# A three-layer float16-pair kernel: GpSimd's elementwise work moved to VectorE and ScalarE

## The chip, the cores and the metric

The kernel runs on one core of one Trainium2 chip. The metric is the device time of one execution in microseconds (us); less is better. Engines are named as in the profile: PE (TensorE matmul), DVE (VectorE), ACT (ScalarE), POOL (GpSimd), SP (SyncE, which here only issues DMAs).

## The reference

The inputs are q, k, v (8 x 8 heads x 576 tokens x 64), a norm weight, and two pairs of float64 weight matrices (512 x 2048 and 2048 x 512).

```python
kv = einsum('bhsd,bhse->bhde', k, v)
out = einsum('bhsd,bhde->bhse', q, kv)
x = out / sqrt(mean(out * out) + 1e-6) * g_norm        # 4608 tokens x 512
h = x @ w_in;   x = (h * sigmoid(1.702 * h)) @ w_out   # layer 0
h = x @ w2_in;  x = (h - tanh(h)) @ w2_out             # layer 1
```

## The kernel before

**Numbers as pairs.** Every operand of the two dense layers is split into a float16 high part and a float16 low part; a product is three float16 matmuls (high-high, high-low, low-high) of 128 x 128 by 128 x 288. The weights arrive as float64 words and are put together on the chip: `words` scales the upper word (line 153 on ACT for layer 0, line 155 on POOL for layer 1), then three DVE instructions (lines 158, 159, 161) shift and merge the bits. ACT casts the result to the high part (lines 187, 212), and `low_part` (line 177) subtracts it from the float32 value.

**Strassen's scheme.** From the second superblock on, each matrix product is done with seven block products in place of eight (Winograd's form). That needs four sums of the weight quadrants: `four` (lines 170 to 173). In layer 0 the sums are made after the first superblock, from the pairs that are already there: `sums_in` and `sums_out` first add high and low part again (lines 228, 246: the pair recombination), then call `four`, cast (lines 234, 256) and subtract. In layer 1 `conv1` does words, sums, cast and low part for 32 pieces and keeps the pairs in DRAM. The moving operand needs three differences and one more in place, in `xprep` (line 315, four instructions per half), then its pairs (lines 325 on ACT, 328 on DVE).

**Superblocks.** 4608 tokens are eight superblocks of 576 per layer. Superblock 0 of layer 0 runs without Strassen's scheme: `m1_plain` (lines 723 to 725) while weights are still being converted by `conv0` in small places of SBUF (st, jt, cbk, xo, gt), then `m2_plain` (lines 756 to 758, operands by lines 739 on ACT and 740 on DVE, in a ring of three). `sums` begins inside `m2_plain`. Superblocks 1 to 7 and all of layer 1 run `m1` (lines 520 to 522; copies out of PSUM at 553 on ACT, additions at 558 on DVE, activations at 527/531) and `m2` (lines 692 to 694; operands by 581 on DVE, 595 on ACT, 601 on DVE; results by 646 on ACT and 640 on DVE).

**Side work.** Beside superblock n of layer 0 runs the attention of superblock n+1: `front` (matmuls 382, 390, 413; squares 401 on ACT, their fp32r copy 404 and remainder 405 on DVE), `roots`, `newton`, and `back` (matmul 448, product 452 on DVE, then `xprep`). `xprep` of superblocks 2 to 6 does line 315 on POOL. From superblock 2 on `conv1` is a second strand. POOL also issues the DMAs of `conv1` and the stores of the results.

**What sets the order.** Side work is written as generators that `tick` advances by fixed rates at each step of the main work; the framework then schedules the program by its own timeline. Each engine executes its queue strictly in that order: an instruction that waits holds all behind it. The rates are not touched by the change, but the order within each queue comes out differently.

## Time and profile before

| | |
|---|---|
| median of three runs | 1568.98 us (1566.72 to 1574.88) |
| span of the profiled execution | 1565.8 us |
| PE, DVE, ACT, POOL busy | 94%, 77%, 58%, 32% of the span |
| POOL busy, all but 25 us of it in the first half | 501.9 us |
| layer 1 begins (first line 520 of its first superblock) | 815.6 us |

The profile gives the time of the profiled execution as its span, from the first to the last instruction; the median of the runs is 3.2 us above it. Busy shares are averages over very unlike stages: superblock 0 (to 188 us), superblock 1 with the rest of the weight sums (to 306 us), superblocks 2 to 7 with attention and `conv1` (to 816 us), and layer 1.

### The profile page before, as it was taken

The page shows a single profiled execution, that of the slowest core. Times are in us where ns is not written, and L with a number is a line of the kernel's source. Part 1 is how long each engine was busy: PE and PEld are TensorE (multiplying, and loading weights), DVE is VectorE, ACT ScalarE, POOL GpSimd, SP SyncE. Part 2 cuts the span into 40 slices and gives each one's busy share as a digit, 9 for nine tenths or more (in the row PEclk, how much of TensorE's full clock was granted, in tenths as well). Part 3 has the DMA queues.
Part 4 walks back from the last instruction along what each step waited for, and adds up shares of the span by engine and source line. Part 5 has one row for each costly group of instructions (what it writes and reads, how often), then busy time and mean ns, then how long its engine had stood idle before and what let it go on. Part 6 is the DMA issues. An engine that isn't in the chain of part 4 may idle for free.

```text
span 1565.8 us, 29411 instructions
## 1 busy us (share of the span) xinstructions
PE 1467.6 (94%) x11508; PEld 1157.2 (74%) x11508; DVE 1205.1 (77%) x2037; ACT 909.4 (58%) x1979; POOL 501.9 (32%) x565
## 2 busy tenths in 40 slices
PE   6969689989999898999999999999999999999998
PEld 5747467767777677777777777777777777777777
DVE  6996998488587696896967777787878786878585
ACT  6655376565665565666646555655655565656463
POOL 2599842165675665745440000000000000000000
PEclk7979899999999999999999999999999999999999
DMA  8673422617647457366475615243343425150604
GB/s 304 186 211 103 142 94 96 237 41 233 217 126 229 152 161 249 105 230 217 122 234 181 234 62 167 76 139 119 116 135 98 144 77 166 52 168 18 202 15 152
DMA packets 88907, 235.34 MB, mean 150 GB/s; under 512 B 9664, under 2 KB 41536, under 8 KB 88768
## 3 DMA queue, kind: packets, MB, share of 16 engines
q1 hardware_dynamic: 75264, 184.30, 36.8%
q0 software_dynamic: 13504, 49.16, 9.3%
q8 instruction: 90, 1.47, 0.4%
q14 instruction: 49, 0.40, 0.1%
HBM read 191.48 MB, written 41.94 MB: 149 GB/s over the span
## 4 chain that ended last, share of the span: by engine, by line
issue 31%; PE 26%; DVE 21%; DMA 8%; POOL 8%; ACT 4%; SPq 1%; DVEq 0%; POOLq 0%; ACTq 0%
DVE gt L581 4%; DVE jt L601 4%; PE X L520 3%; PE X L522 2%; PE X L521 2%; PE X L694 2%; PE X L693 2%; PE X L692 2%; DVE xo L328 2%; DVE mscratch L558 2%; POOL cbk L170 1%; DMA wod<-cbk 1%; PE Y L692 1%; PE Y L693 1%; PE Y L694 1%
## 5 line engine op out<-in xcount | busy, mean ns | idle before, releaser
L601 DVE SCALAR_TENSOR_TENSOR jt<-gt,jt 128x576 f16<-128x576 f32 x420 | 335.2, 808 | 110.1 <-ACT jt L595 106.3
L595 ACT ACTIVATE jt<-gt 128x576 f16<-128x576 f32 x420 | 282.2, 681 | 140.3 <-PE X L694 50.4
L520 PE MATMUL X<-xo,wi 128*128 128x288 f16 x960 | 276.1, 288 | 9.8 <-ACT mscratch L553 6.9
L692 PE MATMUL X<-jt,st 128*128 128x288 f16 x960 | 274.0, 286 | 4.0 <-ACT mscratch L646 3.0
L522 PE MATMUL X<-xo,wi 128*128 128x288 f16 x960 | 275.9, 287 | 0.0
L521 PE MATMUL X<-xo,wi 128*128 128x288 f16 x960 | 275.8, 287 | 0.0
L693 PE MATMUL X<-jt,st 128*128 128x288 f16 x960 | 274.4, 286 | 0.4 <-DVE jt L601 0.4
L694 PE MATMUL X<-jt,st 128*128 128x288 f16 x960 | 274.3, 286 | 0.0
L521 PEld LDWEIGHTS <-wi 128*128 128x128 f16 x1680 | 165.2, 98 | 73.7 <-issue 30.6
L520 PEld LDWEIGHTS <-wi 128*128 128x128 f16 x1680 | 165.1, 98 | 48.3 <-ACT wi L234 4.4
L553 ACT COPY mscratch<-X 128x288 f32<-128x288 f32 x360 | 140.5, 394 | 101.9 <-PE X L522 88.4
L693 PEld LDWEIGHTS <-st 128*128 128x128 f16 x1680 | 164.4, 98 | 47.3 <-issue 4.4
L637 POOL DMA_DIRECT2D outT<-mscratch x28 | 20.0, 714 | 558.9 <-DVE mscratch L640 519.8
L692 PEld LDWEIGHTS <-st 128*128 128x128 f16 x1680 | 164.4, 98 | 46.9 <-DMA st<-wod 4.8
L694 PEld LDWEIGHTS <-st 128*128 128x128 f16 x1680 | 164.4, 98 | 45.6 <-issue 3.5
L522 PEld LDWEIGHTS <-wi 128*128 128x128 f16 x1680 | 165.2, 98 | 42.6
L581 DVE TENSOR_TENSOR gt<-gt 128x576 f32<-128x576 f32 x240 | 188.2, 796 | 1.3 <-ACT gt L527 0.5
L520 PE MATMUL Z<-xo,wi 128*128 128x288 f16 x480 | 138.1, 288 | 18.6 <-DVE mscratch L558 14.6
L558 DVE TENSOR_TENSOR mscratch<-Z,mscratch 128x288 f32<-128x288 f32 x240 | 108.0, 451 | 44.2 <-ACT mscratch L553 26.8
L693 PE MATMUL Y<-jt,st 128*128 128x288 f16 x480 | 136.8, 286 | 2.2 <-DVE jt L601 2.0
L521 PE MATMUL Z<-xo,wi 128*128 128x288 f16 x480 | 138.3, 288 | 0.0
L522 PE MATMUL Z<-xo,wi 128*128 128x288 f16 x480 | 138.2, 288 | 0.0
(255 smaller groups left out, 2970.1 us busy)
## 6 DMA issues: line engine op xcount, KB each, us to landing
st<-wod SPq DMA_DIRECT2D x210, 512.0 KB, 4.7
scratch<-att SPq DMA_DIRECT2D x28, 928.0 KB, 6.6
x2d<-mscratch POOLq DMA_DIRECT2D x32, 288.0 KB, 5.1
scratch<-x2d SPq DMA_DIRECT2D x32, 288.0 KB, 5.8
cbk<-w_out POOLq DMA_DIRECT2D x32, 256.0 KB, 4.2
cbk<-w_in POOLq DMA_DIRECT2D x32, 256.0 KB, 4.3
outT<-mscratch POOLq DMA_DIRECT2D x28, 288.0 KB, 4.8
wid<-cbk POOLq DMA_DIRECT2D x16, 448.0 KB, 3.7
```

The source lines that it names most:

```text
L328: nc.vector.scalar_tensor_tensor(out=dst[:, a:b, 1, :], in0=src, scalar=SX, in1=dst[:, a:b, 0, :], op0=ALU.mult, op1=ALU.subtract)
L520: nc.tensor.matmul(out=out, lhsT=wh, rhs=xh, start=fresh and kt == 0, stop=False, skip_group_check=k)
L521: nc.tensor.matmul(out=out, lhsT=wh, rhs=xl, start=False, stop=False, skip_group_check=k)
L522: nc.tensor.matmul(out=out, lhsT=wl, rhs=xh, start=False, stop=kt == 1, skip_group_check=k)
L553: main(nc.scalar.copy(out=b.ap, in_=x))
L558: main(nc.vector.tensor_tensor(out=b.ap, in0=add[0], in1=b.ap, op=ALU.add))
L581: tt = lambda o, a, b: main(nc.vector.tensor_tensor(out=G[:, :, o, :], in0=G[:, :, a, :], in1=G[:, :, b, :], op=ALU.subtract))
L595: main(nc.scalar.activation(out=j[:, :, 0, :], in_=GT[STEPS2[i][1]][:, :, QD[STEPS2[i][0]], :], func=AF.Copy, scale=SX))
L601: main(nc.vector.scalar_tensor_tensor(out=j[:, :, 1, :], in0=GT[STEPS2[i][1]][:, :, QD[STEPS2[i][0]], :], scalar=SX, in1=j[:, :, 0, :], op ...
L692: nc.tensor.matmul(out=out, lhsT=wh, rhs=xh, start=a, stop=False, skip_group_check=k)
L693: nc.tensor.matmul(out=out, lhsT=wh, rhs=xl, start=False, stop=False, skip_group_check=k)
L694: nc.tensor.matmul(out=out, lhsT=wl, rhs=xh, start=False, stop=z, skip_group_check=k)
```

## The change

All arithmetic leaves POOL, which keeps its few set-up copies and the DMA issues:

- scaling of words (line 155, 32 of 128x512) goes to ACT, as it already was for layer 0;
- `four`, `low_part` and the pair recombination (lines 170 to 173, 177, 228, 246) go to DVE wherever they were on POOL;
- the four subtractions of `xprep` for superblocks 2 to 6 (line 315, 40 of 128x288) go to DVE;
- the fp32r copy of the squares (line 404, 32 of 128x576 on DVE) is replaced by a second Square on ACT that writes fp32r from PSUM (64 of 128x288). Line 405 keeps its subtraction.

DVE's queue goes from 2039 to 2359 instructions, ACT's from 1981 to 2077, POOL's from 570 to 185. PE executes the same matmuls.

```diff
     def words(l, raw, wb):
...
-        if l == 0:
-            nc.scalar.activation(out=av, in_=rf[:, :, 1], func=AF.Copy, scale=2.0 ** -111)
-        else:
-            nc.gpsimd.tensor_scalar(out=av, in0=rf[:, :, 1], scalar1=2.0 ** -111, scalar2=None, op0=ALU.mult)
+        nc.scalar.activation(out=av, in_=rf[:, :, 1], func=AF.Copy, scale=2.0 ** -111)
...
-    def four(Q, E, l=0, e=None):
+    def four(Q, E, l=0):
...
-        tt = (e or nc.gpsimd).tensor_tensor
+        tt = nc.vector.tensor_tensor
...
-    def low_part(d, src, on_pool):
-        e = nc.gpsimd if on_pool else nc.vector
-        e.tensor_tensor(out=d[..., 1, :], in0=src, in1=d[..., 0, :], op=ALU.subtract)
+    def low_part(d, src):
+        nc.vector.tensor_tensor(out=d[..., 1, :], in0=src, in1=d[..., 0, :], op=ALU.subtract)
...
-            low_part(d, x, True)
+            low_part(d, x)
...
-            low_part(d, B[:, 1:8], k % 2)
+            low_part(d, B[:, 1:8])
...
-            nc.gpsimd.tensor_tensor(out=Q[:, h], in0=d[:, h, 0:4, 0, :], in1=d[:, h, 0:4, 1, :], op=ALU.add)
+            nc.vector.tensor_tensor(out=Q[:, h], in0=d[:, h, 0:4, 0, :], in1=d[:, h, 0:4, 1, :], op=ALU.add)
...
-                nc.gpsimd.tensor_tensor(out=x, in0=d[:, :, 0, :], in1=d[:, :, 1, :], op=ALU.add)
+                nc.vector.tensor_tensor(out=x, in0=d[:, :, 0, :], in1=d[:, :, 1, :], op=ALU.add)
...
-            nc.gpsimd.tensor_tensor(out=Q, in0=r[:, :, 0, :], in1=r[:, :, 1, :], op=ALU.add)
+            nc.vector.tensor_tensor(out=Q, in0=r[:, :, 0, :], in1=r[:, :, 1, :], op=ALU.add)
...
-        low_part(r, Q, on_pool)
+        low_part(r, Q)
...
-        tt = lambda o, a, b: e.tensor_tensor(out=o, in0=a, in1=b, op=ALU.subtract)
+        tt = lambda o, a, b: nc.vector.tensor_tensor(out=o, in0=a, in1=b, op=ALU.subtract)
...
                 nc.scalar.activation(out=sq[:, c], in_=A[j][:, 0:H], func=AF.Square)
+                nc.scalar.activation(out=shr[:, c], in_=A[j][:, 0:H], func=AF.Square)
                 nc.scalar.activation(out=og[:, c], in_=A[j][:, 0:H], func=AF.Copy, scale=gsc)
             yield
-            nc.vector.tensor_copy(out=shr, in_=sq)
             nc.vector.tensor_tensor(out=slr, in0=sq, in1=shr.bitcast(F32), op=ALU.subtract)
...
-                yield from xprep(xbs[b, kt], ex, dst[:, kt], nc.gpsimd if 2 <= b <= 6 else nc.vector)
+                yield from xprep(xbs[b, kt], ex, dst[:, kt])
```

Blank lines replace comments in the changed file, and lines are gone, so its numbers run a little lower: 155, 156, 158 are the word instructions 158, 159, 161; 167 to 170 the four sums 170 to 173; 173 the low part 177; 224 and 242 the recombination 228 and 246; 310 is line 315, 323 is 328, 400 is 405, 447 is 452, 553 is 558, 576 is 581, 596 is 601, and 735 is 740.

**Place one: DVE's queue while the last pieces of W_out are converted, beside `m1_plain`** (xo, st, jt and cbk are places of pieces, wi and st the kept pairs). Before:

```order
L158 TENSOR_SCALAR xo_72<-xo_72 128x512
L161 SCALAR_TENSOR_TENSOR cbk<-cbk 128x512 x2
L158 TENSOR_SCALAR xo_72<-xo_72 128x512
L159 SCALAR_TENSOR_TENSOR xo_72<-xo_72 128x512 x2
L161 SCALAR_TENSOR_TENSOR xo_72<-xo_72 128x512 x2
L158 TENSOR_SCALAR st<-st 128x512
L158 TENSOR_SCALAR jt<-jt 128x512
L159 SCALAR_TENSOR_TENSOR st<-st 128x512
L159 SCALAR_TENSOR_TENSOR jt<-jt 128x512
L161 SCALAR_TENSOR_TENSOR st<-st 128x512
```

with the change:

```order
L158 SCALAR_TENSOR_TENSOR xo_72<-xo_72 128x512
L400 TENSOR_TENSOR sq_104<-scratch,sq_103 128x576
L156 SCALAR_TENSOR_TENSOR st<-st 128x512
L155 TENSOR_SCALAR jt<-jt 128x512
L173 TENSOR_TENSOR wi_67<-cbk,wi_67 128x3x128
L173 TENSOR_TENSOR st<-cbk,st 128x128
L173 TENSOR_TENSOR wi_68<-xo_72,wi_68 128x3x128
L173 TENSOR_TENSOR st<-xo_72,st 128x128
L158 SCALAR_TENSOR_TENSOR st<-st 128x512
L173 TENSOR_TENSOR wi_68<-xo_72,wi_68 128x3x128
L156 SCALAR_TENSOR_TENSOR jt<-jt 128x512
L173 TENSOR_TENSOR st<-xo_72,st 128x128
```

The low parts, 128x384 and 128x128 for each piece, now stand between the shifts of the next pieces. From the third to the fourth line 740 (735) DVE has 42 instructions in the old queue and 79 in the new one.

**Place two: DVE's queue at the end of `m2_plain`** (scratch holds the attention of superblock 1, xo its operands; gt is the GELU of superblock 0; line 740 or 735 on gt_76 is the last operand of `m2_plain`). Before:

```order
L452 TENSOR_TENSOR scratch<-AT_88,scratch 128x288
L452 TENSOR_TENSOR scratch<-AT_89,scratch 128x288
L177 TENSOR_TENSOR cbk<-cbk 128x4x128
L315 TENSOR_TENSOR scratch<-scratch 128x288 x2
L740 SCALAR_TENSOR_TENSOR jt<-gt_76,jt 128x2x288
L315 TENSOR_TENSOR scratch<-scratch 128x288
L328 SCALAR_TENSOR_TENSOR xo_72<-scratch,xo_72 128x2x288 x3
L740 SCALAR_TENSOR_TENSOR jt<-gt_76,jt 128x2x288
L328 SCALAR_TENSOR_TENSOR xo_72<-scratch,xo_72 128x288
```

with the change:

```order
L224 TENSOR_TENSOR cbk<-wi_63 128x512
L173 TENSOR_TENSOR cbk<-cbk 128x4x128
L735 SCALAR_TENSOR_TENSOR jt<-gt_76,jt 128x2x288
L310 TENSOR_TENSOR scratch<-scratch 128x288
L224 TENSOR_TENSOR st<-wi_65 128x512
L224 TENSOR_TENSOR cbk<-wi_64 128x512
L167 TENSOR_TENSOR st<-st 128x128
L447 TENSOR_TENSOR scratch<-AT_88,scratch 128x288
L224 TENSOR_TENSOR jt<-wi_66 128x512
L224 TENSOR_TENSOR cbk<-wi_64 128x512
L447 TENSOR_TENSOR scratch<-AT_89,scratch 128x288
```

Before, the attention's products (452) and differences (315) lay ahead of the last line 740. Now six of the eight products and all eight differences of superblock 1 lie behind the last line 735, among weight sums; 63 rows stand from it to the first line 553 of superblock 1 (before, 14).

**Place three: DVE's queue in superblock 4, a piece of `conv1` beside M1.** Before:

```order
L158 TENSOR_SCALAR cbk<-cbk 128x512
L159 SCALAR_TENSOR_TENSOR cbk<-cbk 128x512
L558 TENSOR_TENSOR mscratch<-Y_85,mscratch 128x288
L161 SCALAR_TENSOR_TENSOR cbk<-cbk 128x512
L601 SCALAR_TENSOR_TENSOR jt<-gt_73,jt 128x2x288
L558 TENSOR_TENSOR mscratch<-Z_86,mscratch 128x288
L441 SCALAR_TENSOR_TENSOR sq_104<-sq_103,low,scratch 128x288
L558 TENSOR_TENSOR mscratch<-Z_87,mscratch 128x288
L558 TENSOR_TENSOR mscratch<-Z_86,mscratch 128x288
L452 TENSOR_TENSOR scratch<-AT_88,scratch 128x288
```

with the change:

```order
L156 SCALAR_TENSOR_TENSOR cbk<-cbk 128x512
L553 TENSOR_TENSOR mscratch<-Y_85,mscratch 128x288
L158 SCALAR_TENSOR_TENSOR cbk<-cbk 128x512
L167 TENSOR_TENSOR cbk<-cbk 128x128
L168 TENSOR_TENSOR cbk<-cbk 128x128
L169 TENSOR_TENSOR cbk<-cbk 128x128
L596 SCALAR_TENSOR_TENSOR jt<-gt_73,jt 128x2x288
L170 TENSOR_TENSOR cbk<-cbk 128x128
L553 TENSOR_TENSOR mscratch<-Z_86,mscratch 128x288
L436 SCALAR_TENSOR_TENSOR sq_104<-sq_103,low,scratch 128x288
L173 TENSOR_TENSOR cbk<-cbk 128x7x128
L553 TENSOR_TENSOR mscratch<-Z_87,mscratch 128x288
```

The four sums follow the shifts directly, and every low part (173, 128x7x128) stands in this queue, ahead of line 553; before, every second one did.

## Rows read from the trace of the kernel before

**Rows 1.** The page, part 1: busy time, share of span, instructions, by engine.

```profile
PE 1467.6 (94%) x11508; PEld 1157.2 (74%) x11508; DVE 1205.1 (77%) x2037; ACT 909.4 (58%) x1979; POOL 501.9 (32%) x565
```

**Rows 2.** Busy time by stretch: stretch, length, busy us (instructions) of five engines, PEclk.

```profile
0.00:74.20 74.20, 61.87 (x386) 48.11 (x387) 56.81 (x89) 48.78 (x107) 29.14 (x28) 0.86 0.78 256
74.20:119.20 45.00, 26.70 (x171) 19.71 (x170) 39.45 (x44) 23.49 (x64) 43.41 (x49) 0.73 0.65 188
119.20:181.30 62.10, 49.55 (x373) 38.07 (x371) 49.88 (x49) 30.46 (x59) 57.66 (x81) 0.95 0.33 101
181.30:196.40 15.10, 9.64 (x61) 7.00 (x60) 14.96 (x16) 3.94 (x10) 14.22 (x14) 0.89 0.71 231
196.40:310.70 114.30, 106.09 (x811) 83.61 (x812) 86.51 (x148) 75.51 (x176) 32.84 (x28) 0.99 0.41 140
310.70:815.60 504.90, 470.59 (x3667) 369.42 (x3665) 397.76 (x628) 309.04 (x673) 301.08 (x336) 0.99 0.56 179
```

The order of the busy columns is PE, PEld, DVE, ACT, POOL; behind the clock stand the DMA share and GB/s.

**Rows 3.** The same view, one superblock of layer 1.

```profile
1148.80:1231.30 82.50, 82.50 (x674) 65.72 (x672) 64.37 (x125) 46.88 (x101) 2.86 (x4) 1.00 0.37 119
```

**Rows 4.** Waits of PE, 188 to 816 us: total us, times, longest.

```profile
PE Z L520 <- DVE mscratch L558: 14.6, 11, 2.4
PE AT L413 <- DVE sq L404: 6.8, 7, 2.1
PE X L520 <- ACT mscratch L553: 5.5, 6, 2.1
PE Z L520 <- ACT wi L234: 3.9, 1, 3.9
```

**Rows 5.** Waits, 108 to 189 us; then PE's longest before that.

```profile
DVE jt L740 <- ACT jt L739: 14.8, 5, 5.6
...
PE Y L723 <- ACT gt L726: 11.7, 1, 11.7
```

**Rows 6.** DVE by line, 41 to 49.5 us, POOL idle: busy us, mean ns.

```profile
L159 DVE SCALAR_TENSOR_TENSOR gt<-gt 128x512 uint32<-128x512 uint32 x2 | 1.4, 678 | 0.0
L158 DVE TENSOR_SCALAR cbk<-cbk 128x512 uint32<-128x512 uint32 x2 | 0.8, 414 | 0.0
```

**Rows 7.** DVE by line, 74 to 119 us, POOL 96% busy.

```profile
L159 DVE SCALAR_TENSOR_TENSOR cbk<-cbk 128x512 uint32<-128x512 uint32 x4 | 4.5, 1153 | 0.0
L158 DVE TENSOR_SCALAR cbk<-cbk 128x512 uint32<-128x512 uint32 x4 | 3.5, 896 | 0.0
```

**Rows 8.** DVE timeline: start us, us; spacing of starts without idle between.

```profile
66.43 0.68 DVE L159 SCALAR_TENSOR_TENSOR jt<-jt 128x512 uint32<-128x512 uint32 x1
67.03 0.68 DVE L159 SCALAR_TENSOR_TENSOR gt<-gt 128x512 uint32<-128x512 uint32 x1
...
195.77 0.41 DVE L170 TENSOR_TENSOR st<-st 128x256 f32<-128x256 f32 x1
196.10 0.41 DVE L171 TENSOR_TENSOR cbk<-cbk 128x256 f32<-128x256 f32 x1
```

**Rows 9.** DVE by line, 240 to 810 us: busy, mean ns, idle before.

```profile
L601 DVE SCALAR_TENSOR_TENSOR jt<-gt,jt 128x576 f16<-128x576 f32 x162 | 141.8, 887 | 30.7 <-ACT jt L595 29.7
L581 DVE TENSOR_TENSOR gt<-gt 128x576 f32<-128x576 f32 x92 | 79.2, 867 | 0.6
L558 DVE TENSOR_TENSOR mscratch<-Z,mscratch 128x288 f32<-128x288 f32 x87 | 38.6, 448 | 16.1 <-ACT mscratch L553 13.7 <-PE Z L522 2.0
L177 DVE TENSOR_TENSOR cbk<-cbk 128x896 f16<-128x896 f32 x16 | 18.0, 1125 | 17.3 <-ACT cbk L212 17.3
```

**Rows 10.** DVE by line, 810 to 1566 us, where POOL does no arithmetic.

```profile
L601 DVE SCALAR_TENSOR_TENSOR jt<-gt,jt 128x576 f16<-128x576 f32 x254 | 189.6, 754 | 77.0 <-ACT jt L595 74.2
L581 DVE TENSOR_TENSOR gt<-gt 128x576 f32<-128x576 f32 x144 | 105.5, 749 | 0.2
L558 DVE TENSOR_TENSOR mscratch<-Z,mscratch 128x288 f32<-128x288 f32 x144 | 65.4, 454 | 28.1 <-PE Z L522 13.5 <-ACT mscratch L553 13.0
L315 DVE TENSOR_TENSOR scratch<-scratch 128x288 f32<-128x288 f32 x64 | 26.3, 449 | 0.1
```

**Rows 11.** ACT by line, 240 to 810 us: busy, mean ns, idle before.

```profile
L212 ACT CAST cbk<-cbk 128x896 f16<-128x896 f32 x32 | 30.0, 938 | 76.0 <-POOL cbk L173 75.9
L401 ACT ACTIVATE scratch<-AT 128x288 f32<-128x288 f32 x40 | 16.3, 408 | 5.8 <-PE AT L390 5.7
```

**Rows 12.** ACT by line, whole span: the scaling of words.

```profile
L153 ACT ACTIVATE cbk<-cbk 128x512 f32<-128x512 f32 x10 | 6.7, 680 | 0.9 <-DMA cbk<-w_out 0.9
```

More of the change, by code (lines that the diff above doesn't have):

```diff
@@ L227, in sums_in @@
         for h in range(2):
-            nc.gpsimd.tensor_tensor(out=Q[:, h], in0=d[:, h, 0:4, 0, :], in1=d[:, h, 0:4, 1, :], op=ALU.add)
+            nc.vector.tensor_tensor(out=Q[:, h], in0=d[:, h, 0:4, 0, :], in1=d[:, h, 0:4, 1, :], op=ALU.add)
         yield
-        four(Q, Q, e=nc.vector)
+        four(Q, Q)
         yield
@@ L236, in sums_in, with sums_out @@
         for h in range(2):
-            low_part(d[:, h, 3:7], Q[:, h], False)
+            low_part(d[:, h, 3:7], Q[:, h])
         yield
-    def sums_out(p, h, on_pool, at, held):
+    def sums_out(p, h, at, held):
         r = at[:, 0:512].bitcast(F16).rearrange("p (s t f) -> p s t f", s=4, t=2)
@@ L263, in sums @@
     def sums():
-        act, i = [], 0
+        act = []
         while act or todo_in or todo_out or not closed:
@@ L278, in sums @@
                     p, h = todo_out.pop(0)
-                    g, k = sums_out(p, h, i % 2, at, p not in gone), 1
-                i += 1
+                    g, k = sums_out(p, h, at, p not in gone), 1
                 next(g)
@@ L308, in main, with xprep @@
         latest[ins.ins.engine] = ins.ins
-    def xprep(xb, ex, dst, e=nc.vector):
+    def xprep(xb, ex, dst):
         B = xb.ap.rearrange("p (s f) -> p s f", s=4)
         E = ex.ap.rearrange("p (s f) -> p s f", s=3)
-        tt = lambda o, a, b: e.tensor_tensor(out=o, in0=a, in1=b, op=ALU.subtract)
+        tt = lambda o, a, b: nc.vector.tensor_tensor(out=o, in0=a, in1=b, op=ALU.subtract)
         tt(E[:, 0, :], B[:, 1, :], B[:, 0, :])
```

## The prediction

> **What bounds the kernel now.** I read the page's busy line first: PE is busy 94% of 1565.8 us, DVE 77%, POOL 32% [rows 1]. Then the busy times stage by stage, which say where that average hides something. A superblock of layer 1 takes 82.5 us with PE busy for all of it [rows 3]: there PE alone is the bound, POOL does no arithmetic, and the change can win or lose nothing. So all of it happens before 815.6 us. There PE idles 8.2 us of 114.3 in superblock 1, 34.3 us of 504.9 in superblocks 2 to 7, and much more before: from 74.2 to 119.2 us DVE is busy 39.45 us of 45.0 and POOL 43.41, PE 26.70 [rows 2]. In that stretch PE waited 11.7 us at once for one GELU [rows 5], which stood in ACT's queue behind casts of weight pieces, and those waited for DVE's shifts. Superblock 0 is bound by DVE and POOL, not by PE.
>
> The reader should see next that DVE's own durations depend on POOL. Line 159 takes 678 ns while POOL is idle and 1153 ns while POOL is 96% busy; line 158 takes 414 and 896 ns [rows 6, 7]. The operand lines 601 and 581 take 887 and 867 ns in superblocks 2 to 7, 754 and 749 ns in layer 1; line 558, which reads PSUM, is alike in both, 448 and 454 ns [rows 9, 10]. So part of DVE's 77% is POOL's doing, on instructions with both inputs in SBUF.
>
> Here a rule of the Trainium skill speaks against the change: the page "Perfetto Trace Analysis", section "Optimizing Scalar/DVE Operations", says that with DVE saturated it may pay to give work to ScalarE or even GpSimd, though it adds that moving between DVE and GpSimd may not help as they share a port. The change does the opposite of the first half. By it alone the moved work would be a pure addition, the rival "no relief" below. The rows side with the second half.
>
> **Prices on an undisturbed DVE.** Two starts of line 159 without idle between lie 0.60 us apart, two of a 256-column sum 0.33 us [rows 8]. On that line 128 columns cost 0.20 us, 288 cost 0.37, 384 cost 0.47, 576 cost 0.67, 896 cost 1.00 (estimates from those two spacings); line 158, 0.08 us less than its 414 ns, 0.34. That a float16 input costs the same on DVE I take from nothing nearer than line 177's float16 output; at half or double the price its 20 us (16 of 512 columns, 16 of 384 + 128) would be 10 or 40, which the range below is meant to hold.
>
> **The sum, by stretches between marks in DVE's queue.** From the order of the changed queue I count what stands between the same two instructions.
>
> Up to the third line 740 (74.2 us). DVE is busy 56.81 us; the rest is first loads and attention. Low parts come in (0.60 each), the fp32r copies go, POOL's disturbance goes. But that operand needs GELU results that PE delivers at its own pace, so little can be had: -4 us (0 to -8).
>
> From there to the fourth line 740 (45.0 us), where W_out is converted. New queue: 14 line 158 at 0.34, 16 and 18 shifts and merges at 0.60, 14 low parts of 384 and 14 of 128, two of 512, two of 576 columns: 4.8 + 20.4 + 6.6 + 2.8 + 1.2 + 1.3 = 37.1 us. The old queue had 15 such merges, no low part, and took 39.45 us for them. Behind the last merge the old queue idled 5.6 us for line 739 on ACT, its longest wait [rows 5], and that remains, since line 739 needs the first step of `m2_plain`. 37.1 + 5.6 = 42.7: -2.3 us (-8 if the wait goes, +3 if DVE waits for casts ahead of its low parts).
>
> To the last line 740 (62.1 us), `m2_plain`. New queue: 12 line 740, 15 recombinations of 384 + 128, 56 sums of 128 columns, 14 low parts of 512, and some 6.5 us of small things: 8.0 + 10.0 + 11.2 + 8.4 + 6.5 = 44 us, so PE's 49.55 us of work bind. Before, line 740 waited 14.8 us in this stage [rows 5] and ran under a POOL busy for 57.66 us. I take 52 us: -10 (0 to -13).
>
> To the first line 558 of superblock 1 (15.1 us). Here it turns. Six products 452, all eight differences 315 and the eight operand instructions 328 of superblock 1 now stand behind the last operand of `m2_plain`, mixed with 8 recombinations, 28 sums and 9 low parts: 2.2 + 3.0 + 4.8 + 4.8 + 0.7 + 8.3 + 5.4 + 0.7 = 29.9 us, plus some 3 us of hand-overs to ACT and PE. PE has a few steps left and then nothing. 33 against 15.1: +18 us (+15 to +21).
>
> Together +1.7 us: superblock 0 gives back at its end what it wins.
>
> Superblock 1 (114.3 us). The sums that were late are done, among them PE's 3.9 us wait for a cast [rows 4]; PE's own 106.1 us bound it. -4 us (+3 to -7).
>
> Superblocks 2 to 7 (504.9 us). Added on DVE: 32 differences at 0.37, 128 sums at 0.20, 16 more low parts at 1.00: 11.8 + 25.6 + 16 = 53 us. Taken off: 20 copies 404 (11 us) and POOL's disturbance, 162 line 601 and 92 line 581 by 0.13 and 0.12 us, with the other SBUF lines in like proportion some 45 us. DVE's load stays where it was. What changes is waiting. ACT stood 75.9 us, 26 times, with its cast 212 at the head of its queue waiting for POOL's sums [rows 11]; copies 553 and operands 595 stood behind it. On DVE four sums cost 0.8 us in a row. Against that, all 32 low parts now wait in DVE's queue for that cast; the 16 that did so waited 17.3 us [rows 9], so some 17 us more. ACT takes 32 scalings at 0.68 [rows 12] and 40 squares at 0.41 [rows 11], 38 us, beside 309.04 of 504.9 busy. PE's waits on lines 558, 404 and 553, 26.9 us from 188 us on [rows 4], are the most that can come back. POOL's queue keeps only DMA issues, with 301.08 us of arithmetic gone from between them [rows 2]; I cost that at nothing, since earlier loads and stores help only `conv1`, which has until the end of the layer; if its loads came late instead, line 155's place on ACT would block the queue as the cast does. I take -10 us, a third of PE's idle time here, between +10 (new waits win) and -25.
>
> Sum: +1.7 - 4 - 10 = -12 us on the span of 1565.8; the median of the runs lies 3.2 us above it. **1569 - 13 = 1556 us.** About 0.5%, 8 us, is what a measurement of this kernel can tell from no change.
>
> **Rivals.** *The hole before superblock 1 decides (slower).* The stretch +18 comes as counted, but `m2_plain` does not shrink: its steps hang on line 739, whose ring slot PE frees, so 62 us stay 62 and the first two stretches stay too; the later superblocks win only 5. 18 + 3 - 5 = +16: 1585 us. With the first two stretches unchanged it decides once `m2_plain` shortens by less than 8 us. For it: PE's clock there is already 0.95, and idle PE lowers it (0.73 from 74 us on [rows 2]). Against: line 740 there runs against a nearly full POOL. 0.13.
>
> *No relief (slower).* DVE's slowness under load has another cause than POOL, and the moved work adds: 59 us in the second stretch in place of 45, 53 us in superblocks 2 to 7, a third of it past DVE's idle time onto PE: +14 + 18 + 10 = +42, 1611 us. Rows 6 and 7 speak plainly against. 0.03.
>
> *Even.* Gains and the hole cancel, and the new waits on casts eat the old ones on POOL: 1561 to 1577, say 1568 us. 0.28.
>
> *ACT's stall was the brake (much faster).* With 75.9 us of blocked ACT gone, PE regains nearly all 26.9 us of those waits and superblock 0 its 14 us without the hole: 1569 - 27 - 12 = 1530 us. 0.11.
>
> **How the numbers follow.** My forecast has 0.45. With the last rival, faster by over 0.5% has 0.56; the even case, 0.28; the two slower ones, 0.16. The range leaves out "no relief", half of the hole and half of the best case: 1533 to 1580.
>
> **What would show it.** Right: line 159 at about 0.68 us throughout superblock 0, lines 601 and 581 near 0.75 us before 815 us; ACT's wait at the cast of `conv1` down from 75.9 to under 25 us; a hole in PE of 15 us or more between the last line 756 and the first 520, waiting for operands xo; superblocks 2 to 5 at 102 to 105 us each. Wrong: DVE waiting more than 40 us for that cast with PE's wait for line 558 over 15 us; a superblock 1 longer than 115 us; layer 1 other than 750 us.

## The result, and the profile after

The changed kernel takes 1520.3 us in the median (1517.85 to 1525.42) against 1569.76 us for the kernel before on the same chip: a ratio of 0.9695, 95% interval 0.9676 to 0.9715. That is 49 us less where 13 were forecast, and outside the forecast's range (1533 to 1580). The direction was right, the size was not. The span fell from 1565.8 to 1516.1 us.

The page of the changed kernel, busy time by engine, against [rows 1]:

```profile
PE 1458.2 (96%) x11508; PEld 1155.3 (76%) x11508; DVE 1186.5 (78%) x2357; ACT 946.1 (62%) x2075; POOL 125.8 (8%) x181
```

POOL lost 376 us of work, most of which DVE took, 320 instructions more; yet DVE is busy 18.6 us *less* (1205.1 before). The chain that ended last, by engine, has PE at 39% where it was 26%, and DVE at 3% where it was 21%:

```profile
PE 39%; issue 18%; DVE 3%; DMA 2%; ACT 1%; POOL 1%; POOLq 0%; ACTq 0%; SPq 0%
```

The windows of the changed kernel, between the same marks in DVE's queue as [rows 2] (third, fourth and last operand of `m2_plain`, first PSUM addition of superblock 1, first of superblock 2, start of superblock 7); columns as there:

```profile
0.00:65.20 65.20, 51.88 (x315) 40.23 (x316) 47.22 (x90) 46.65 (x108) 2.10 (x9) 0.87 0.80 261
65.20:103.90 38.70, 34.96 (x259) 27.23 (x258) 37.46 (x82) 28.81 (x76) 0.00 (x0) 0.91 0.87 268
103.90:148.10 44.20, 43.89 (x348) 34.77 (x347) 44.20 (x128) 26.86 (x55) 1.57 (x2) 1.00 0.47 143
148.10:177.90 29.80, 17.92 (x87) 10.77 (x85) 29.80 (x72) 14.02 (x29) 1.45 (x2) 0.66 0.39 125
177.90:282.20 104.30, 98.39 (x771) 78.61 (x769) 71.87 (x137) 69.79 (x167) 4.71 (x7) 1.00 0.41 140
282.20:766.60 484.40, 468.27 (x3692) 372.33 (x3690) 396.03 (x789) 341.79 (x751) 91.99 (x129) 0.99 0.58 189
```

| stretch | before | forecast | after | change, forecast | change, measured |
|---|---|---|---|---|---|
| to the third operand | 74.2 | 70.2 | 65.2 | -4 | -9.0 |
| to the fourth | 45.0 | 42.7 | 38.7 | -2.3 | -6.3 |
| to the last (`m2_plain`) | 62.1 | 52 | 44.2 | -10 | -17.9 |
| to superblock 1's first addition | 15.1 | 33 | 29.8 | +18 | +14.7 |
| superblock 1 | 114.3 | 110 | 104.3 | -4 | -10.0 |
| superblocks 2 to 6 | 504.9 | 495 | 484.4 | -10 | -20.5 |
| superblock 7 and layer 1 | 750.2 | 750 | 749.5 | 0 | -0.7 |

One label ahead of the prediction is wrong: the mark at 815.6 us is the start of layer 0's superblock 7, and layer 1 begins at 899.7 us (851.2 in the changed kernel). What the forecast calls superblocks 2 to 7 are superblocks 2 to 6, and its layer 1 is superblock 7 and layer 1. Its sums are not touched by that.

Three things are read from the windows. In the second to fourth stretch DVE is busy 37.46 of 38.70, 44.20 of 44.20 and 29.80 of 29.80 us: there it is the bound now, in the third together with PE, which is busy 43.89 of 44.20. In the fourth PE is idle 11.9 of 29.8 us and its granted clock falls to 0.66: the hole that the forecast saw. From superblock 1 on PE is the engine nearest its limit: in superblocks 2 to 6 it is busy 468.27 of 484.40 us, its idle time down from 34.3 to 16.1 us, and DVE's busy time there is what it was (396.03 against 397.76) though it took all of POOL's arithmetic.

That DVE's instructions run undisturbed is seen in its lines, first 65 to 104 us of the changed kernel (a merge and, last, the shift; [rows 7] has 1153 ns for a merge, line 159, and 896 ns for the shift, line 158), then 195 to 765 us, against [rows 9]:

```profile
L158 DVE SCALAR_TENSOR_TENSOR cbk<-cbk 128x512 uint32<-128x512 uint32 x6 | 4.1, 682 | 0.0
...
L155 DVE TENSOR_SCALAR cbk<-cbk 128x512 uint32<-128x512 uint32 x5 | 2.1, 421 | 1.1 <-ACT cbk L152 1.0
```

```profile
L596 DVE SCALAR_TENSOR_TENSOR jt<-gt,jt 128x576 f16<-128x576 f32 x166 | 123.3, 751 | 21.1 <-ACT jt L590 19.9
L576 DVE TENSOR_TENSOR gt<-gt 128x576 f32<-128x576 f32 x94 | 70.0, 750 | 0.1
L553 DVE TENSOR_TENSOR mscratch<-Z,mscratch 128x288 f32<-128x288 f32 x92 | 41.2, 450 | 14.9 <-ACT mscratch L548 9.6 <-PE Z L517 5.1
L173 DVE TENSOR_TENSOR cbk<-cbk 128x896 f16<-128x896 f32 x32 | 34.8, 1087 | 8.2 <-ACT cbk L208 7.9
```

Lines 596 and 576 (601 and 581 before) are at 751 and 750 ns instead of 887 and 867. The 32 low parts on line 173 wait 7.9 us for the cast in all; the forecast had 34. On ACT, same stretch, against [rows 11]:

```profile
L208 ACT CAST cbk<-cbk 128x896 f16<-128x896 f32 x32 | 30.1, 940 | 7.5 <-DVE cbk L170 3.9 <-issue 2.5 <-ACT gt L522 0.7
L152 ACT ACTIVATE cbk<-cbk 128x512 f32<-128x512 f32 x32 | 21.8, 680 | 18.5 <-DMA cbk<-w_in 7.1 <-DMA cbk<-w_out 4.8 <-DVE cbk L173 3.7
L397 ACT ACTIVATE sq<-AT 128x288 fp32r<-128x288 f32 x44 | 18.4, 418 | 0.0
```

ACT's 76.0 us at the cast are 7.5. PE's waits from 173 to 767 us, against [rows 4], show what is left there, loads first of all; the 14.6 us for DVE's PSUM addition (now line 553) are 0.2:

```profile
PE AT L377 <- DMA scratch<-att: 10.4, 8, 2.3
PE X L515 <- ACT mscratch L548: 3.9, 4, 2.4
PE Y L687 <- DMA st<-wod: 3.5, 5, 1.1
...
PE Z L515 <- DVE mscratch L553: 0.2, 1, 0.2
```

### The profile page after: what moved, and what is told of

The parts are those of the page before. It is cut to its first block, busy times and chain, and to the rows that moved or that the text cites. A ratio compares the mean times of both kernels' runs of the same rounds, so it can differ in the third digit from the quotient of the medians.

```text
span 1516.1 us, 29345 instructions
## 1 busy us (share of the span) xinstructions
PE 1458.2 (96%) x11508; PEld 1155.3 (76%) x11508; DVE 1186.5 (78%) x2357; ACT 946.1 (62%) x2075; POOL 125.8 (8%) x181
## 4 chain that ended last, share of the span: by engine, by line
PE 39%; issue 18%; DVE 3%; DMA 2%; ACT 1%; POOL 1%; POOLq 0%; ACTq 0%; SPq 0%
PE X L515 4%; PE X L517 4%; PE X L516 4%; PE X L687 3%; PE X L689 3%; PE X L688 3%; PE Z L515 2%; PE Z L517 2%; PE Z L516 2%; PE Y L687 2%; PE Y L689 2%; PE Y L688 2%; DMA st<-wod 1%; DVE jt L596 1%; DVE gt L576 1%
## 5 line engine op out<-in xcount | busy, mean ns | idle before, releaser
L596 DVE SCALAR_TENSOR_TENSOR jt<-gt,jt 128x576 f16<-128x576 f32 x420 | 313.1, 754 | 96.9 <-ACT jt L590 93.0
L576 DVE TENSOR_TENSOR gt<-gt 128x576 f32<-128x576 f32 x240 | 177.2, 751 | 0.4
L687 PE MATMUL Y<-jt,st 128*128 128x288 f16 x480 | 135.4, 286 | 4.9 <-DMA st<-wod 4.9
L689 PE MATMUL Y<-jt,st 128*128 128x288 f16 x480 | 136.8, 286 | 0.0
```

The costliest lines, as they stand in the source:

```text
L576: tt = lambda o, a, b: main(nc.vector.tensor_tensor(out=G[:, :, o, :], in0=G[:, :, a, :], in1=G[:, :, b, :], op=ALU.subtract))
L596: main(nc.vector.scalar_tensor_tensor(out=j[:, :, 1, :], in0=GT[STEPS2[i][1]][:, :, QD[STEPS2[i][0]], :], scalar=SX, in1=j[:, :, 0, :], op ...
L687: nc.tensor.matmul(out=out, lhsT=wh, rhs=xh, start=a, stop=False, skip_group_check=k)
L689: nc.tensor.matmul(out=out, lhsT=wl, rhs=xh, start=False, stop=z, skip_group_check=k)
```

## The experiments

Three theories stood at first. **Stretching** ("disturbance" in the expectations): POOL's arithmetic lengthens DVE's instructions, and that is what the change takes away. **The stall** ("chain"): ACT's wait at the cast for POOL's sums was the brake. **Order**: the gain comes of the new order of the queues. Stages are compared by the start of TensorE's first product in each: `m1_plain` | `m2_plain` | superblock 1 | superblocks 2 to 6. The kernel before has 78.6 | 80.9 | 117.7 | 509.3 us, the changed one 67.7 | 56.2 | 125.4 | 487.8. (Superblock 1's first products now start before the hole, so its stage holds the hole.) Ratios are against the kernel before, run beside each; intervals are 95%.

### One part alone, on the kernel before

**p1, the first layer's weights on DVE.**

```
-            low_part(d, x, True)
+            low_part(d, x, False)
-        four(Q, Q)
+        four(Q, Q, e=nc.vector)
-        low_part(r, Q, on_pool)
+        low_part(r, Q, False)
...
```

(the three pair recombinations in `sums_in` and `sums_out` likewise on `nc.vector`)

> The kernel before with only layer 0's weight work moved to DVE (low parts, recombination, four sums of W_in and W_out); conv1, the differences of the operands and the squares stay as before. Disturbance: POOL is idle until conv1 begins, so nearly all of the 28 us that superblocks 0 and 1 gained come: 1538 to 1546 us, superblocks 2 to 7 as before. Chain: low parts end their chains, so little of it comes: 1555 to 1565. Order: anything, not adding up with the other parts.

Measured: 1552.4 us, 0.9900 (0.987 to 0.9931); 65.1 | 66.4 | 126.4 | 513.6. The time lies between the two ranges expected. Superblock 0 alone wins 28 us; superblock 1 is 8.7 us longer, the hole.

**p2, the second layer's weights:** scaling on ACT, sums and all low parts on DVE.

```
-        if l == 0:
+        if True:
             nc.scalar.activation(out=av, ...
-            four(B[:, 0:4], B[:, 4:8], 1)
+            four(B[:, 0:4], B[:, 4:8], 1, e=nc.vector)
-            low_part(d, B[:, 1:8], k % 2)
+            low_part(d, B[:, 1:8], False)
```

> The kernel before with only conv1 moved: scaling on ACT, four sums and every low part on DVE. Superblocks 0 and 1 as before (159.5 and 117.7 us between marks). Disturbance: POOL keeps 43 us of line 315, so superblocks 2 to 6 give most of the 21 us that they gained: 1546 to 1554 us, line 601 near 780 ns there. Chain: the same or a little less, with the cast's wait for POOL gone. Parts that don't add up (14.9 us of layer 0's weights are known) speak for order.

Measured: 1560.8 us, 0.9942 (0.9924 to 0.996); 78.6 | 81.2 | 117.6 | 504.4. ACT's wait for POOL at the cast is 0, the operand line is down from 900 to 764 ns in superblocks 2 to 6, and still they win only 4.9 us; the time lies 7 us above the range expected from stretching.

**p3, the operand subtractions.**

```
-                yield from xprep(xbs[b, kt], ex, dst[:, kt], nc.gpsimd if 2 <= b <= 6 else nc.vector)
+                yield from xprep(xbs[b, kt], ex, dst[:, kt], nc.vector)
```

> The kernel before with only the differences of the operands (line 315, superblocks 2 to 6) on DVE: POOL loses 43 us, DVE gains 40 x 0.37 = 15. Disturbance: 15 us for about 43 x 0.3 = 13 us of relief: within 5 us of before. Chain: ACT waits for line 315 on POOL were 3 us in all: within 3 us.

Measured: 1570.0 us, 1.0005 (0.9987 to 1.0023); 78.6 | 81.8 | 119.5 | 508.5. Nothing.

**p4, the squares,** written twice by ACT, with DVE's copy gone.

```
                 nc.scalar.activation(out=sq[:, c], in_=A[j][:, 0:H], func=AF.Square)
+                nc.scalar.activation(out=shr[:, c], in_=A[j][:, 0:H], func=AF.Square)
...
-            nc.vector.tensor_copy(out=shr, in_=sq)
```

> The kernel before with only the fp32r squares on ACT: DVE loses 19 us of line 404, ACT gains 64 x 0.31 = 20 us; PE's 8 us of waits for line 404 go to ACT. Disturbance: no part of it, within 5 us of before (1562 to 1572). If it brings 10 us or more, then the copies were what delayed PE.

Measured: 1575.7 us, 1.0043 (1.003 to 1.0056); 81.8 | 77.6 | 122.2 | 508.9. Slightly slower, and 4 us above the range.

The four ratios add to -1.1%, some 17 us, where the whole change gives 49: the parts do not add.

### Disturbance and lateness added to the changed kernel

**d0** puts 162 marks, a one-column copy on DVE and one on POOL, at the places where POOL worked; it is the control of **d1**, which puts POOL additions of constants into a dead tile behind the marks. Nobody reads them. They are more than POOL had: 504 of 256 or 128 columns, 420 us, where the kernel before has 384 instructions and 384 us.

```
...
+        nc.vector.tensor_copy(out=k, in_=src)
+        nc.gpsimd.tensor_copy(out=hl0[:, 255:256], in_=k)
+        c = sel.bitcast(F32)
+        for n, f16 in ops:       # d0: in ()
+            o = hl0[:, 0:n]
+            nc.gpsimd.tensor_tensor(out=o, in0=c[:, 0:n], in1=c[:, 512:512 + n], op=ALU.add)
...
```

> The changed kernel plus 162 one-column copies on DVE and as many on POOL, one behind each place where POOL used to work; the control for the next run. All theories: DVE loses 162 x about 0.1 us = 16 us of queue time, most of it in superblocks 0 to 7 beside idle time of DVE: 1520 to 1532 us, line 601 (596 in the changed kernel) at 754 ns in superblocks 2 to 7.

> The same, and behind each of these copies POOL adds columns of a constant tile, about as many and as large as the work that the change took from it, into a place that nobody reads. No other engine waits for POOL. Theory 'disturbance' (POOL's work slows DVE's instructions with two SBUF inputs, and that was the cost): line 601 back to 850 to 900 ns in superblocks 2 to 7, and 25 to 45 us over the control. Rival 'chain' (POOL's results came late, and ACT and DVE stood in their queues waiting for them): within 5 us of the control, whatever the durations. Rival 'order' (the new queue order is the gain): within 10 us of the control.

Measured: d0 1537.0 us, 0.9766 to 0.983; 68.3 | 56.8 | 135.8 | 492.4, so the marks themselves cost 17 us, mostly in superblock 1; the time is 5 us above the range expected. d1 1653.4 us, 1.0501 to 1.0573; 68.2 | 85.8 | 157.8 | 553.8. In 240 to 840 us DVE's operand line is stretched and its PSUM line is not:

```profile
L622 DVE SCALAR_TENSOR_TENSOR jt<-gt,jt 128x576 f16<-128x576 f32 x144 | 126.4, 887 | 13.2 <-ACT jt L616 12.7
...
L579 DVE TENSOR_TENSOR mscratch<-Z,mscratch 128x288 f32<-128x288 f32 x86 | 37.8, 445 | 15.2 <-ACT mscratch L574 14.1 <-PE Z L543 1.0
```

Those are the numbers of the kernel before, with no DVE instruction waiting for POOL. `m2_plain` goes back to 85.8 us (80.9 before) with DVE busy throughout; `m1_plain` got only some 13 us of the additions and shows nothing. For that stage the trace of the kernel before speaks, 29 to 108 us: DVE busy 77.05 of 79.00 us, so that its stretched instructions were the bound there.

```profile
29.00:108.00 79.00, 61.18 (x423) 45.97 (x423) 77.05 (x99) 50.84 (x119) 56.56 (x50) 0.82 0.72 215
```

The size of the loss in d1 (116 us over d0, where 25 to 45 were expected) is not a clean price: the dose is larger than POOL's own, and `conv1`'s loads and stores are issued by POOL and queue behind the additions.

**d2** and **d3** make the stall without the stretching: ACT's cast waits for a chain of 20, or 70, POOL fills of one column.

```
             four(B[:, 0:4], B[:, 4:8], 1)
+            nc.gpsimd.tensor_copy(out=gs, in_=B[:, 7, 0:1])
+            for _ in range(20):      # d3: 70
+                nc.gpsimd.memset(gs, 0.0)
+            nc.gpsimd.tensor_copy(out=B[:, 7, 0:1], in_=B[:, 7, 0:1])
```

> The changed kernel with conv1's cast made to wait for POOL again: behind the four sums on DVE POOL does a one-column copy, 20 one-column memsets and a one-column copy in place, about 2.4 us that read next to nothing; 32 pieces. Theory 'chain': ACT waits at the cast 50 to 80 us in superblocks 2 to 7 as before, and the time rises by 10 to 20 us to 1530 to 1540, durations unchanged. Theory 'disturbance': the wait comes back, but the time stays within 5 us of 1520, line 601 at 754 ns.

> As the late-sums run, with 70 memsets in place of 20 (about 7 us a piece), so that ACT's wait at the cast reaches or passes the 76 us of the kernel before; in the first run it was 20.7 us for 4 us of time. Chain: 15 us or more over the changed kernel, 1536 us and up. Disturbance: under 10 us, 1520 to 1530.

Measured: d2 1524.3 us (0.9687 to 0.9758), superblocks 2 to 6 at 494.2, ACT's wait 20.7 us where 50 to 80 were meant. d3 1543.0 us (0.9813 to 0.9869), 506.6, wait 43.0 us. The operand line in d3, 278 to 790 us, with POOL busy 208 us on its fills:

```profile
L600 DVE SCALAR_TENSOR_TENSOR jt<-gt,jt 128x576 f16<-128x576 f32 x140 | 103.8, 752 | 18.6 <-ACT jt L594 17.9
```

So the stall is real too: 43 us of it come with a loss of 19 (in d2, 20.7 us with 6.4). In d3 DVE's instructions also come in another order, which was not tried apart; in d2 the order is nearly that of the changed kernel. And a busy POOL as such does not stretch DVE; one-column fills leave the line at 752 ns. Where DVE was stretched, POOL worked on 128 to 896 columns; whether it is the width or the reading of operands in SBUF that counts was not tried apart.

### One part taken out of the whole change

Each leaves one part as it was before (the edits of p1 to p4, applied but for one).

> The whole change but for the squares, which stay as before (one copy on VectorE). Moved alone the squares gave +6 us, and the four parts alone sum to -16 where the change gives -49; something is gained only together. Theory A, each moved part takes a brake off and the last brake standing sets the pace: the squares matter little once POOL is quiet, superblock 0's two stretches at about 68 and 59 us (after: 67.7 and 56.2), superblocks 2 to 6 at 490 (487.8), total 1522 to 1530. Theory B, the joint gain hangs on the attention chain that the squares shorten: superblocks 2 to 6 stay near 500 and the total is 1535 or more.

> The whole change but for the operand subtractions of superblocks 2 to 6, which stay on POOL (35 us of POOL work in superblocks 2 to 6 as in the run of the second layer's weights alone, where the eviction with operands in SBUF took 764 ns). Theory A, brakes in series: the subtractions alone on POOL disturb little, eviction 755 to 770 ns, superblocks 2 to 6 at 490 to 494, total 1522 to 1528. Theory B, POOL's latency on the operands of M1 was the hidden brake: superblocks 2 to 6 near 500, PE waiting for xo, total 1532 or more. Superblock 0 as after in both (68 and 57).

> The whole change but for the second layer's weights, which stay on POOL: ScalarE waits some 70 us for POOL at the cast and the eviction takes about 870 ns while POOL works. Theory A: superblocks 2 to 6 lose nearly the whole gain, 503 to 510 us, total 1536 to 1545, superblock 0 as after (68 and 57). Theory B, that the joint gain lies elsewhere (fewer instructions in ScalarE's queue, the squares): superblocks 2 to 6 at 495 or less, total 1530 or less.

> The whole change but for the first layer's weights, which stay on POOL. Superblock 0 as before or a little better (about 79 and 78 us; squares alone gave 82 and 78), superblock 1 at 118 to 122 without the hole ahead of it, superblocks 2 to 6 at 488 to 495 if they depend on the second layer's weights and their neighbours alone (theory A), total 1550 to 1560. Theory B, the queue's order left by superblock 0 (weights' sums emitted later) is what helps superblocks 2 to 6: 503 to 509, total 1568 or more.

| left as before | us | ratio, interval | stages | lost against the whole change |
|---|---|---|---|---|
| squares (u1) | 1529.6 | 0.9713 to 0.9779 | 67.5, 64.1, 128.5, 492.7 | 9 |
| subtractions (u2) | 1542.4 | 0.9805 to 0.9853 | 66.2, 57.9, 129.5, 506.4 | 22 |
| second layer's weights (u3) | 1548.7 | 0.9846 to 0.9888 | 66.8, 58.3, 125.9, 512.5 | 28 |
| first layer's weights (u4) | 1538.2 | 0.9775 to 0.9827 | 81.8, 77.5, 119.5, 478.0 | 18 |

Taken out, the parts are worth 77 us in sum (by the medians); put in alone, 17. The subtractions show it best: alone they are worth nothing, last they are worth 22 us. In u3 ACT's stall is back (280 to 800 us):

```profile
L212 ACT CAST cbk<-cbk 128x896 f16<-128x896 f32 x32 | 30.0, 938 | 65.8 <-POOL cbk L173 63.6 <-DMA x2d<-mscratch 2.1
```

In u2 it is not, and still superblocks 2 to 6 are at 506.4. Theory A (490 to 494) was wrong there; the number is nearer theory B's, but its cause is not seen: no wait of PE for xo is among PE's nine longest, and d6 below tries the lateness apart. u4 shows the price of a quick superblock 0: where it takes 35 us longer, superblocks 1 to 6 take 16 us less, all of it in superblocks 1 and 2: superblock 1 is without the hole, and superblock 2 has less of the attention left to do (84 attention products of PE in its trace against 102 in that of the changed kernel). Its time, like its superblocks 2 to 6, lies below both ranges expected. u1's total lies in theory A's range, u3's 4 us above it.

### The pair, and what the subtractions on POOL cost by

**p23** moves the second layer's weights and the subtractions on the kernel before (the edits of p2 and p3).

> The kernel before with two parts moved: the second layer's weights and the operand subtractions. Alone they gave superblocks 2 to 6 504.4 and 508.5 us (before 509.3), and taking either out of the whole change gave 506 and 512. Theory A, two brakes of which either alone is enough: both away together give most of what the whole change gives there, superblocks 2 to 6 at 478 to 490, superblock 0 and 1 as before (79, 81, 118), total 1540 to 1550. Theory B, all four parts are needed: superblocks 2 to 6 at 498 or more, total 1556 or more.

Measured: 1544.4 us, 0.9826 (0.9787 to 0.9865); 78.6 | 81.1 | 119.9 | 482.5. The pair gives 26.8 us in superblocks 2 to 6 where its halves gave 4.9 and 0.8: theory A of that text.

**d4** and **d5** leave the subtractions on DVE and add POOL subtractions that nobody reads, four or eight for each operand; **d6** instead holds the operands' casts back by a chain of 40 fills of one column.

```
         tt(E[:, 2, :], B[:, 2, :], E[:, 1, :])
+        if n:                        # d4: 4 for superblocks 2 to 6; d5: 8
+            nc.gpsimd.tensor_copy(out=hl0[:, 0:1], in_=E[:, 0, 0:1])
+            for _ in range(n):
+                nc.gpsimd.tensor_tensor(out=hl0, in0=sel.bitcast(F32)[:, 0:H], in1=sel.bitcast(F32)[:, H:2 * H], op=ALU.subtract)
...
+        if late:                     # d6 alone, superblocks 2 to 6
+            nc.gpsimd.tensor_copy(out=gs, in_=E[:, 2, 0:1])
+            for _ in range(40):
+                nc.gpsimd.memset(gs, 0.0)
+            nc.gpsimd.tensor_copy(out=E[:, 2, 0:1], in_=E[:, 2, 0:1])
```

> The whole change, and at the places of the operand subtractions of superblocks 2 to 6 POOL does four subtractions of 288 columns for each operand that nothing reads (40 in all, about 35 to 45 us of POOL time), besides those on VectorE. Theory A, the stretching of VectorE's instructions is the brake that the subtractions on POOL put on: VectorE's same instructions take some 15 to 20 us more in superblocks 2 to 6 (17.3 in the run without this part) and those superblocks take 500 to 507 us, total 1533 to 1540. Theory B, the brake is the wait of the operands on POOL's slower subtractions and its queue: 488 to 493, total 1521 to 1526.

> The same with eight for each operand, 80 in all, about 70 to 90 us of POOL time. Theory A: the excess on VectorE doubles to 30 to 40 us and the superblocks 2 to 6 take 510 to 525 us, total 1545 to 1560. Theory B: 488 to 495, total 1521 to 1530.

> The whole change, with the casts of each superblock's operands (2 to 6) held back by a chain of POOL instructions on one column (a copy, 40 fills of 101 ns, a copy: some 5 us, against 2.5 us that four subtractions of 1.08 us on POOL take longer than on VectorE) which read no wide operand. Latency of the operands alone, without stretching. If stretching is the whole brake: superblocks 2 to 6 at 487 to 492, VectorE's excess under 2 us, total 1518 to 1526. If the latency brakes too: 496 or more, total 1530 or more.

Measured: d4 1541.0 us (0.9791 to 0.9842), superblocks 2 to 6 at 503.9. d5 1560.4 us (0.9929 to 0.9972), 527.6; its profiled execution lies 10 us above its median, so that stage reads high. d6 1520.6 us (0.9671 to 0.9727), 484.8, the same as the changed kernel. DVE's instructions stand in d4 and d5 in exactly the order of the changed kernel, so order has no part in what they lose; their times are theory A's, at the upper end or just over. Lateness of the operands costs nothing; stretching alone (d4) costs 16.1 of the 18.6 us that u2 loses there. POOL's lines in u2 (270 to 800 us) and in d4 give the dose, 34.6 and 33.5 us:

```profile
L315 POOL TENSOR_TENSOR scratch<-scratch 128x288 f32<-128x288 f32 x32 | 34.6, 1091 | 21.0 <-DVE scratch L452 20.3
```

```profile
L319 POOL TENSOR_TENSOR hl<-sel 128x288 fp32r<-128x288 f32 x32 | 33.5, 1048 | 2.2
```

What it does to DVE in d4, 286 to 790 us (the changed kernel has 671 and 446 ns for the first two lines, 449 for the third), and last the wait of PE by which it reaches the time (0.2 us in the changed kernel):

```profile
L327 DVE SCALAR_TENSOR_TENSOR xo<-scratch,xo 128x576 f16<-128x576 f32 (+1 forms) x40 | 27.7, 696 | 0.0
L310 DVE TENSOR_TENSOR scratch<-scratch 128x288 f32<-128x288 f32 x40 | 23.8, 614 | 0.0
...
L557 DVE TENSOR_TENSOR mscratch<-Z,mscratch 128x288 f32<-128x288 f32 x80 | 35.8, 449 | 7.9 <-ACT mscratch L552 7.3 <-PE Z L521 0.6
```

```profile
PE Z L519 <- DVE mscratch L557: 8.6, 7, 2.2
```

Summed over all groups of DVE instructions in superblocks 2 to 6 (count times mean less the mean of the changed kernel), the stretching is 47.5 us in the kernel before, 16.2 in p2, 17.3 in u2, 16.1 in d4, 31.9 in d5, 34.5 in p3, 1.3 in p23, 1.2 in d3, under 1 in d6.

Why halves don't add is seen in PE's idle time. All rows are of superblocks 2 to 6, in us; the waits are PE's waits for DVE and for ACT, the stall is ACT's wait for POOL at the cast.

| | length | PE idle | waits for DVE, ACT | stretching | stall |
|---|---|---|---|---|---|
| before | 509.3 | 34.3 | 20.3, 12.5 | 47.5 | 75.9 |
| p3 | 508.5 | 31.8 | 16.4, 10.9 | 34.5 | 71.4 |
| p2 | 504.3 | 31.4 | 10.9, 11.1 | 16.2 | 0 |
| u2 | 506.4 | 32.5 | 10.9, 8.8 | 17.3 | 0 |
| d4 | 503.9 | 29.3 | 9.2, 8.1 | 16.1 | 0 |
| d3 | 506.6 | 30.9 | 4.1, 17.5 | 1.2 | 43.0 |
| p23 | 482.5 | 13.2 | 0.2, 4.0 | 1.3 | 0 |
| the change | 487.8 | 16.1 | 0.2, 4.1 | 0 | 0 |
| d6 | 484.8 | 15.4 | 0.2, 5.3 | under 1 | 0 |

With either brake on, or both, PE idles 29 to 34 us; with neither, 13 to 16. Where it is lost is read from the first halves of superblocks 2 to 6 (`m1`, where the side work on the next operands and on `conv1` meets the PSUM additions that PE waits for; from the first product of `m1` to its last X products): the last row of the windows over those five stretches, first their length, then busy time. Before; p2; p23; the changed kernel; u2; d4; d6; d3:

```profile
sum 260.10, PE 239.12 PEld 186.48 DVE 205.89 ACT 170.46 POOL 166.02; mean PE 47.82 PEld 37.30 DVE 41.18 ACT 34.09 POOL 33.20
```

```profile
sum 251.50, PE 236.21 PEld 185.79 DVE 213.62 ACT 179.19 POOL 83.41; mean PE 47.24 PEld 37.16 DVE 42.72 ACT 35.84 POOL 16.68
```

```profile
sum 237.50, PE 234.90 PEld 187.08 DVE 203.86 ACT 184.65 POOL 42.12; mean PE 46.98 PEld 37.42 DVE 40.77 ACT 36.93 POOL 8.42
```

```profile
sum 243.30, PE 237.68 PEld 188.73 DVE 204.36 ACT 183.73 POOL 43.88; mean PE 47.54 PEld 37.75 DVE 40.87 ACT 36.75 POOL 8.78
```

```profile
sum 256.80, PE 240.35 PEld 189.17 DVE 217.76 ACT 181.20 POOL 82.60; mean PE 48.07 PEld 37.83 DVE 43.55 ACT 36.24 POOL 16.52
```

```profile
sum 261.20, PE 241.81 PEld 190.00 DVE 219.79 ACT 184.36 POOL 79.78; mean PE 48.36 PEld 38.00 DVE 43.96 ACT 36.87 POOL 15.96
```

```profile
sum 244.20, PE 237.03 PEld 188.15 DVE 201.54 ACT 181.73 POOL 84.56; mean PE 47.41 PEld 37.63 DVE 40.31 ACT 36.35 POOL 16.91
```

```profile
sum 248.30, PE 235.18 PEld 185.00 DVE 198.55 ACT 173.81 POOL 149.87; mean PE 47.04 PEld 37.00 DVE 39.71 ACT 34.76 POOL 29.97
```

In the six where the cast does not wait for POOL, the length is DVE's busy time and 34 to 43 us more: 213.6 goes with 251.5, 203.9 with 237.5, 204.4 with 243.3, 217.8 with 256.8, 219.8 with 261.2, 201.5 with 244.2. The two with the stall stand off: the kernel before, 205.9 with 260.1, and d3, 198.6 with 248.3, 54 and 50 us more. There the stall adds. So p2 takes the stall away but gives DVE 7.7 us more in these halves, and most of the gain is spent; moving the subtractions then takes 9.8 off DVE and 14 off the length, though DVE now does them itself: the stretching that goes with them (16.2 us in p2) is more than their own time (32 times 446 ns, 14.3 us), and some other work of DVE falls into the second halves. The subtractions alone (p3) leave the stall in place and win nothing in all: their first halves take 244.9 us (DVE 193.7, again 51 us apart), 15 less than before, but their second halves 14 more, and why was not looked into. Two brakes, either enough to hold the pace.

One thing is left over. u2 loses 13.5 us in the first halves and 5 more in the second, where its POOL does no arithmetic; what carries those 5 was not found.

### Two attempts at a faster version

**o2** sends the weights' sums of superblock 0 more slowly, so that superblock 1's attention and operands come earlier in DVE's queue.

```
-                    dfr.append(add_side(sums(), 1.5, 0.7))
+                    dfr.append(add_side(sums(), 1.5, 0.4))
```

> The whole change with the weights' sums emitted at rate 0.4 instead of 0.7 beside the plain second product, so that VectorE does superblock 1's attention and operands sooner. If the sums ahead of those operands make the hole in superblock 1 (125.4 us against 117.7 before), it closes: superblock 0 and 1 together at 240 to 245 instead of 249.3, total 1511 to 1517. If VectorE's whole work up to there sets the time (251 us of work in those 249 us), nothing is gained: 247 to 251, total 1518 to 1524.

Measured: 1532.2 us, 0.976 (0.9734 to 0.9787); 67.8 | 55.6 | 132.4 | 493.8. Slower than the change by some 12 us and above both ranges: superblock 1 grows by 7, superblocks 2 to 6 by 6. Sending the sums later does not close the hole. That DVE's work up to there has to be done in any order would explain it, but that was not tried apart.

**x1** puts three steps of side work between a superblock's first attention load and the product that reads it.

```
         nxt = None if places else (yield from load(b, 0))
+        if nxt is not None:
+            yield
+            yield
+            yield
```

> The whole change, with three steps of side work between the load of a superblock's first attention unit and its first product, on which TensorE waited 8.4 us in six places (2.3 us each at most). If those waits are on TensorE's path: they go, 4 to 8 us less, total 1512 to 1516. If another engine's chain takes over or the attention that now comes three steps later is late at its superblock's end: 1518 to 1526.

Measured: 1531.7 us, 0.9756 (0.9729 to 0.9782); 66.8 | 63.9 | 121.5 | 498.0. The time is above both ranges, and the edit missed its aim: PE's wait for those loads, 290 to 770 us, is no shorter (8.7 us, against 8.4 in the changed kernel).

```profile
PE AT L381 <- DMA scratch<-att: 8.7, 6, 3.3
PE AT L389 <- ACT kv L385: 5.1, 2, 4.6
```

So whether those waits are on the path stays open. No version tried beats the changed kernel.

## Why the prediction was wrong in size

**Right: the mechanism on DVE.** Merges at 682 to 686 ns throughout superblock 0 (forecast about 0.68 us), lines 596 and 576 at 751 and 750 ns (0.75), DVE's load in superblocks 2 to 6 unchanged, ACT's wait at the cast 7.5 us (under 25), superblock 7 and layer 1 unchanged. The Trainium skill's page "Perfetto Trace Analysis", section "Optimizing Scalar/DVE Operations", offers GpSimd as a relief for a saturated DVE and adds that the two share a port, so that it may not help. This case agrees with the second half and goes further: 34.6 us of subtractions on POOL stretched DVE's other work by 17.3 us (u2), and doing them on DVE costs 32 times 446 ns, 14.3 us.

**Failed: the step "behind the last merge the old queue idled 5.6 us for line 739 on ACT ... and that remains".** It went: 38.7 us against a packed queue of 37.1. DVE had no wait on that line left from 65 to 178 us. In the old trace line 739 waited 4.1 of those 5.6 us for a step of `m2_plain`, as the forecast says; but that step had waited 3.5 us for a GELU, and the GELU stood on ACT behind two casts that had waited 4.0 us for DVE's stretched merges on line 161. So the wait went with the stretching; that is read from the order of the queues, and no run tried it apart. (The "15 such merges" of the old queue were 28, 13 on line 159 and 15 on line 161; no sum hangs on it.)

**Failed most in superblock 0: the step for `m2_plain`, "44 us, so PE's 49.55 us of work bind", from which "I take 52 us".** The stretch took 44.2 us, DVE's packed sum to 0.2 us; the trace has the instructions that were counted, 12 operands, 15 recombinations, 56 sums and 14 low parts of 512 columns. PE's work was not tied to the marks in DVE's queue: with GELUs less late (PE's wait for one is 3.7 us in place of 11.7) PE did 34.96 us in the stretch before (26.70 in the kernel before), 43.89 here, and 17.92 in the stretch behind (9.64). The forecast took an engine's work in a window of the old kernel as its floor in the new one.

**Right in size, wrong in weight: the hole.** "29.9 us, plus some 3 us" was measured at 29.8, with PE idle 11.9 us; the trace has the instructions counted, six products, eight differences, 28 sums and nine low parts among them, so this is no luck. It stands inside superblock 1's first products, not ahead of them as the text said (TensorE's last product of `m2_plain` and its first of superblock 1 lie 1.8 us apart). The rival that let it decide needed `m2_plain` to shorten by less than 8 us; it shortened by 17.9. The four stretches gave -18.5 instead of +1.7.

**Too small: superblock 1 (-4; measured -10.0) and superblocks 2 to 6 (-10; measured -20.5).** For superblock 1 the step was "PE's own 106.1 us bound it", the same mistake again: PE was busy 98.39 us in the new stretch. For the later ones the term was "a third of PE's idle time"; more than half came back, 18.2 of 34.3 us. Two of its parts were mis-sized. DVE's new wait for the cast was put at 17 us more, "all 32 low parts now wait"; it fell from 17.3 to 7.9. The cast that the low part waits for no longer waits for POOL itself (76.0 us before, 7.5 now); that this is the reason is read from the two lines and was not tried apart. And stretching and stall were weighed as one sum to be shared among waits. They are two brakes on the same half of a superblock, and only a change that takes both off, as this one does, gets the whole. Superblocks 4 and 5 took 97.1 and 95.8 us, not 102 to 105; superblock 2, at 109.2, still carries attention that superblock 0 left behind (u4: 98.1).

The rival "ACT's stall was the brake" came nearest with 1530 us, but by half of the cause: p2 takes that stall away and wins 9 us, d3 puts 43 us of it back and loses 23. For the squares the runs settle only the numbers: +7 us alone, -9 as the last part, by a way that was not looked into. In u1's profiled execution, which lies 5 us above its median, half of the loss stands in `m2_plain` (64.1 against 56.2).
